# A forward and backward decode kernel: five wq chunks kept in SBUF, w1's place lent to other loads, w2's chunks released one step earlier

## The chip, the cores and the metric

The kernel runs on one core of one Trainium2 chip. The metric is the time of one execution on the device in microseconds (us); lower is better. A run's profile is one execution, taken by the hardware profiler.

## What is computed

Two attention layers A and two dense layers B alternate, for one token, and the gradient of all of it with respect to the input, both caches and all weights is computed as well. Both attention layers use the same wq, wo and caches, and both dense layers the same w1, b1 and w2, so every gradient of a weight is a sum over two layers.

```python
# D = 1024, Hq = 32, Hkv = 4, Dh = 128, Sk = 32768, F = 3584; all bfloat16
def A(x, k_cache, v_cache, wq, wo):
    W = 4096                                  # only the last 4096 positions are read
    q = x @ wq
    p = softmax(q . k[Sk-W:] * Dh ** -0.5)
    return (p @ v[Sk-W:]) @ wo                # wq: D x 4096, wo: 4096 x D
def B(x, w1, b1, w2):
    h = x @ w1 + b1
    return (h * tanh(softplus(h))) @ w2       # w1: D x F, w2: F x D
x = x + A(ln(x)); x = x + B(ln(x)); x = x + A(ln(x)); x = x + B(ln(x))
# outputs: x, then grad_out pulled back to x, k_cache, v_cache, wq, wo, w1, b1, w2
```

Of the gradients of the caches only the last 4096 of 32768 positions differ from zero. The rest, 56 pieces of 1 MiB, is written as zeros.

## The kernel before

**Stages.** The order is: transposes of K and attention forward 0 (`attn_fwd`), dense forward 0 (`mlp_fwd`, then a loop over the seven chunks of w2 with `mlp_out`), attention forward 1, dense forward 1, then backward: `dn_b1` (through w1 of layer B1), `attn_bwd(1)`, a loop over w2's seven chunks that does the forward product of layer B1 and the backward product of layer B0 together, `dn_b0`, `attn_bwd(0)`, and last the gradients of all weights and caches (`units_rows`, `units_cols`, `units_kv`), which are computed from short rows and written out. The program's order on each engine is written by hand.

**Chunks and the ring.** wq has 8 chunks, wo 8, w2 7, each 1 MiB; w1 has 8 tiles of 0.875 MiB. K's four groups and V's four are 1 MiB each. `Ring` (L38) holds 8 slots of 1 MiB. `want` puts a load at the end of one list; `pump` issues loads from the head of the list on SP's queue as long as there is a free slot, and stops at the first that finds none; `release` frees a slot and pumps. A load with a place of its own (`own`) takes no slot. A key such as ("2", 0, 3) names chunk 3 of w2 for use 0; the text writes it 2(0,3). wq is used four times (q(0,t) and q(1,t) forward, q(2,t) and q(3,t) backward), wo three times (o(0,c), o(1,c), o(3,c)), w2 twice. `keep` renames a slot's chunk to its next use, so that it isn't loaded again: KEEP_Q for q(1,t), KEEP_Q2 for q(3,t).

**Turning.** A backward product needs a weight's blocks transposed. `turned` (L426) does it in place: 8 PE transposes (L431) into PSUM, a copy back by ACT or DVE (`evac`, L284 and L287), and later the product itself (L443). `later` and `flush` delay the products: up to two (in attn_bwd up to six) stay open behind the newest transposes. A row may instead be multiplied on DVE (`rowdot`, L408). In `rows_chunk` two of the four rows of a w2 chunk go to DVE, two are turned. A chunk of q(2,t) that is kept for q(3,t) stays turned.

**Zeros.** `zeros(n, after)` issues n of the 56 zero writes on GpSimd's queue (POOL, L248). With `after` it first copies one element of that tile, so that POOL waits for it; what comes later on POOL waits too.

**Results.** In the last stage `stage_free` is a list of 1 MiB places in which results are put together before SP stores them (L967, L972). They are the third of w1's place that is left over (3 places), then V's and K's places and the ring's.

Of the kernel before, what the change touches and what calls it, by code (L numbers as in the profile page):

```python
# [15 lines left out]
P = 128  # L16
HQ = 32
DH = 128
D = 1024
J = 4096  # L20
F = 3584
G = 4
W = 4096
TD = D // P
TF = F // P
TS = W // P
SLOT = 4096
# [10 lines left out]
class Ring:  # L38
# [6 lines left out]
        self.pending = deque()  # L45
        self.where = {}

    def want(self, key, src, shape, own=None):
        self.pending.append((key, src, shape, own))

    def pump(self):
        while self.pending:
            key, src, shape, own = self.pending[0]
            if own is None:
                if not self.free:
                    return
                s = self.free.popleft()
                n = 1
                for k in shape[1:]:
                    n *= k  # L60
                dst = self.slots[s][:, 0:n]
                if len(shape) == 3:
                    dst = dst.rearrange("p (a b) -> p a b", a=shape[1])
                self.where[key] = (s, dst)
            else:
                dst = own
            self.pending.popleft()
            self.nc.sync.dma_start(dst, src)

# [6 lines left out]

    def release(self, key):
        s, _ = self.where.pop(key)
        self.free.append(s)
        self.pump()  # L80


# [1 line left out]
def kernel(  # L84
# [50 lines left out]
    W1 = sb([P, TD, F], BF16, "W1")  # L135
# [55 lines left out]
    DQC = sb([P, HQ, 2], BF16, "DQC")  # L191
# [14 lines left out]
    ring = Ring(nc, [ring_t[:, i, :] for i in range(8)])  # L206
    wq_v = A_wq.rearrange("(t p) j -> p t j", p=P)

    wo_v = A_wo.rearrange("(c p k) d -> p c k d", p=P, k=4)
# [3 lines left out]
    def kv_src(cache, g):  # L213
        return cache[0, g, ZR:, :].rearrange("(p t) d -> p t d", p=P)
# [2 lines left out]
        for t in ts:  # L217
            ring.want(("q", k, t), wq_v[:, t, :], [P, J])

    def want_o(k, cs=range(8)):  # L220
        for c in cs:
            ring.want(("o", k, c), wo_v[:, c], [P, 4, D])

    def want_2(k, cs=range(7)):
        for c in cs:
# [14 lines left out]
    def zeros(n, after=None):  # L240

        if after is not None and zjobs:
            nc.gpsimd.tensor_copy(pz[0:1, pz_n[0] % 16:pz_n[0] % 16 + 1], after[0:1, 0:1])
            pz_n[0] += 1
        for _ in range(n):
            if zjobs:
                dst = zjobs.pop()
                nc.gpsimd.dma_start(dst, zt[:])  # L248


    KEEP_Q = (6, 7)
    KEEP_Q2 = (5, 6, 7)
    EARLY_2 = (0, 1)
    for g in range(G):
        ring.want(("K", g), kv_src(A_k_cache, g), [P, TS, P])
    want_q(0)
    for g in range(G):
        ring.want(("V", g), kv_src(A_v_cache, g), None, own=VS[:, g])
    want_2(0, EARLY_2)
    want_o(0)  # L260
    for t in range(TD):
        ring.want(("1", t), w1_v[:, t, :], None, own=W1[:, t, :])
    want_2(0, [c for c in range(7) if c not in EARLY_2])
    want_q(1, [t for t in range(8) if t not in KEEP_Q])
    want_o(1)
# [157 lines left out]
    def flush():  # L423
        while lag:
            lag.popleft()[1]()
# [169 lines left out]
    def mlp_fwd(l, x, st):  # L595
        name = f"B{l}"
        n32, rstd = ln_fwd(x, st, NB[:, :, l], name)
        h_ps = MV[:, 192:192 + TF]
        for t in range(TD):
            for fb in range(TF):  # L600
                nc.tensor.matmul(h_ps[:, fb:fb + 1], lhsT=f_block(W1[:, t], fb), rhs=NB[:, t, l:l + 1],  # L601
                                 start=(t == 0 and fb == 0), stop=(t == TD - 1), skip_group_check=True)

        taken = []

        def col(n):
            if n == "mp":
                return sb([P, TF], FP32, f"{n}_{name}")
            taken.append(n)
            return mlp_t[:, (len(taken) - 1) * TF:len(taken) * TF]  # L610

        h, nh, z, w, m, om, A, B, num, den, t_, = (col(n) for n in "h nh z w m om A B num den t".split())
        V = nc.vector
        V.tensor_tensor(out=h[:], in0=h_ps, in1=b1c[:], op=ALU.add)

        V.scalar_tensor_tensor(out=nh[:], in0=h[:], scalar=-1.0, in1=h[:], op0=ALU.mult, op1=ALU.min)
        nc.scalar.activation(z[:], nh[:], ACT.Exp)
        nc.scalar.activation(w[:], nh[:], ACT.Exp, scale=2.0)
        V.tensor_scalar(out=m[:], in0=h[:], scalar1=0.0, scalar2=None, op0=ALU.is_ge)
        V.tensor_scalar(out=om[:], in0=h[:], scalar1=0.0, scalar2=None, op0=ALU.is_lt)  # L620
        V.tensor_tensor(out=A[:], in0=m[:], in1=w[:], op=ALU.max)
        V.tensor_tensor(out=B[:], in0=om[:], in1=w[:], op=ALU.max)
        V.scalar_tensor_tensor(out=num[:], in0=z[:], scalar=2.0, in1=A[:], op0=ALU.mult, op1=ALU.add)
        V.scalar_tensor_tensor(out=den[:], in0=B[:], scalar=2.0, in1=num[:], op0=ALU.mult, op1=ALU.add)
        V.reciprocal(den[:], den[:])
        V.tensor_tensor(out=t_[:], in0=num[:], in1=den[:], op=ALU.mult)
        if l == 0:
            V.tensor_tensor(out=AC[:, :, l], in0=h[:], in1=t_[:], op=ALU.mult)

        def deriv():  # L630

            mp, sg, s2 = col("mp"), col("sg"), col("s2")
            V.tensor_scalar(out=s2[:], in0=z[:], scalar1=1.0, scalar2=None, op0=ALU.add)
            V.reciprocal(s2[:], s2[:])
            V.tensor_tensor(out=sg[:], in0=m[:], in1=z[:], op=ALU.max)
            V.tensor_tensor(out=sg[:], in0=sg[:], in1=s2[:], op=ALU.mult)
            V.tensor_tensor(out=mp[:], in0=t_[:], in1=t_[:], op=ALU.mult)
            V.tensor_scalar(out=mp[:], in0=mp[:], scalar1=-1.0, scalar2=1.0, op0=ALU.mult, op1=ALU.add)
            V.tensor_tensor(out=mp[:], in0=mp[:], in1=h[:], op=ALU.mult)
            V.tensor_tensor(out=mp[:], in0=mp[:], in1=sg[:], op=ALU.mult)  # L640
            V.tensor_tensor(out=mp[:], in0=mp[:], in1=t_[:], op=ALU.add)
            return mp

        def act_late():
            V.tensor_tensor(out=AC[:, :, l], in0=h[:], in1=t_[:], op=ALU.mult)

        return dict(n32=n32, rstd=rstd, deriv=deriv, act_late=act_late)

    def mlp_out(l, ch, c, y_ps):
        for tt in range(4):  # L650
            fb = 4 * c + tt
            for dd in range(TD):
                nc.tensor.matmul(y_ps[:, dd:dd + 1], lhsT=ch[:, tt, dd * P:(dd + 1) * P], rhs=AC[:, fb, l:l + 1],
                                 start=(fb == 0 and dd == 0), stop=(fb == TF - 1), skip_group_check=True)
# [37 lines left out]
            early_da(2 * c + 1)  # L692

    x1, st1, sA0 = attn_fwd(0, x0, st0, True, wo_hook0)
    sB0 = mlp_fwd(0, x1, st1)
    mp0 = sB0["deriv"]()
    y_ps = MV[:, 256:256 + TD]
    mv_open()
    for c in range(7):
        ch = ring.get(("2", 0, c))  # L700
        mlp_out(0, ch, c, y_ps)
        if c in EARLY_2:
            ring.release(("2", 0, c))
        elif c < 6:
            rows_chunk(ch, c, GB, 1, gbc, da1, DA)
            later(lambda c=c: ring.release(("2", 0, c)))
# [32 lines left out]
    x3, st3, sA1 = attn_fwd(1, x2, st2, False, wo_hook1, last_da)  # L739
    put_by("OC", OC, HQ)  # L740
    put_by("NA", NA, TD)
    zeros(7, x3)
    sB1 = mlp_fwd(1, x3, st3)
    put_by("NB", NB, TD)
    conv(8, "A")
# [175 lines left out]

    def dq3():
        w1_rest(2)
        zeros(3, DQC[:, 0, 1:2])

    def dn3(t):
        if t % 2:
            w1_rest(1)
        if t == 5:
            zeros(1, dnp[:, t:t + 1])  # L930

    g2 = attn_bwd(1, sA1, g3, ("o", 1), ("q", 2), KEEP_Q2,
                  dict(do=lambda c: conv(2), dp=dp3, dq=dq3, dn=dn3))


    W1S = W1[:].rearrange("p t f -> p (t f)")
    ROWS = W1S[:, 0:5120]
    NOFF = 1024
    rf = W1S[0:7, 5120:6144]
# [3 lines left out]
    DOST = W1S[:, 11008:11264]  # L943

    TWIN = W1S[:, 11264:16384]
    stage_free = deque(W1S[:, 16384 + i * SLOT:16384 + (i + 1) * SLOT] for i in range(3))
    rt_n = [0]

    def rowize(cols, n, base, off):
# [118 lines left out]


    nc.vector.tensor_copy(GB[:, :, 0], g2[:])  # L1070
    zeros(3, g2)
    bcast(lambda c: GB[:, c, 0:1], TD)
    da0 = tmp([P, HQ], FP32, "da")
    y_ps = MV[:, 384:384 + TD]
# [2 lines left out]
    for c in range(7):  # L1077
        ch = ring.get(("2", 1, c))
        mlp_out(1, ch, c, y_ps)
        rows_chunk(ch, c, GB, 0, LB[0], da0, DA)  # L1080
        later(lambda c=c: ring.release(("2", 1, c)))
    flush()
# [3 lines left out]
    w1_rest(len(w1_units))  # L1086
    zeros(2, dh0)
    g1 = dn_b0(g2)
    nc.vector.tensor_copy(GA[:, :, 0], g1[:])
    zeros(2, g1)  # L1090

    x4 = sb([P, TD], BF16, "x4")
    nc.vector.tensor_tensor(out=x4[:], in0=y_ps, in1=x3[:], op=ALU.add)
# [8 lines left out]
    def do1(c):  # L1102
        if c == 0:
            rowize(GA, TD, 32, 0)
        if c == 3:
            todo[1].append(units_rows(32, HQ, out_5))
        if c == 5:
            store_rows(x4[:], TD, out_0[0, 0, :])
            store_f(db)
        if c == 5:  # L1110
            zeros(1, do1_acc[:, 4 * c:4 * c + 1])

    def dp1():
        zeros(4)
# [7 lines left out]

    def dn1(t):
        if t in (3, 6, 7):
            zeros(2 if t < 7 else 1, dnp[:, t:t + 1])
        if t == 4:
            twins()
        if t == 5:
            todo[0].append(units_cols(0, 8, out_4))
# [9 lines left out]
    nc.vector.tensor_copy(g0b[:], g0[:])  # L1139
    store_rows(g0b[:], TD, out_1[0, 0, :])  # L1140
    stage_free.extendleft(ring_t[:, i, :] for i in range(8))

    way.close()
    late = ctx.enter_context(tc.tile_pool(name="late", bufs=1, space=bass.MemoryType.PSUM))
# [42 lines left out]
```

## Time and profile before

| | before |
|---|---|
| time, median of 3 runs (lowest, highest) | 461.11 us (460.48, 461.47) |
| span of the profiled execution | 460.6 us |
| busy share: PE, PE weight load, DVE, ACT, POOL | 73%, 60%, 57%, 50%, 8% |
| moved by DMA | 183.59 MB, 399 GB/s on average |
| of it zero writes on POOL's queue | 58.72 MB |
| read from HBM, written to it | 83.94 MB, 98.62 MB |

The profiled execution's own time is not given apart from its span; the median of the three runs is 0.5 us above that span. "PE" is the matrix engine, "DVE" the vector engine, "ACT" the scalar engine, "SP" the queue that issues most DMAs. In a timeline a row is: start, duration, engine, line, operation, output and input, count, and in brackets the idle time before it and what ended it. In a row of a window follow its length, the busy time (and count) of PE, PE's weight loads, DVE, ACT and POOL, then the granted clock of PE, the share of DMA time and GB/s.

### The profile page before, as it was taken

The page shows a single profiled execution, that of the slowest core. Times are in us where ns is not written, and L with a number is a line of the kernel's source. Part 1 is how long each engine was busy: PE and PEld are TensorE (multiplying, and loading weights), DVE is VectorE, ACT ScalarE, POOL GpSimd, SP SyncE. Part 2 cuts the span into 40 slices and gives each one's busy share as a digit, 9 for nine tenths or more (in the row PEclk, how much of TensorE's full clock was granted, in tenths as well). Part 3 has the DMA queues.
Part 4 walks back from the last instruction along what each step waited for, and adds up shares of the span by engine and source line. Part 5 has one row for each costly group of instructions (what it writes and reads, how often), then busy time and mean ns, then how long its engine had stood idle before and what let it go on. Part 6 is the DMA issues. An engine that isn't in the chain of part 4 may idle for free. (4 is left out here: it accounts for less than half of the span.)

```text
span 460.6 us, 14273 instructions
## 1 busy us (share of the span) xinstructions
PE 337.2 (73%) x6385; PEld 275.3 (60%) x6385; DVE 261.3 (57%) x517; ACT 228.2 (50%) x263; POOL 38.6 (8%) x85
## 2 busy tenths in 40 slices
PE   4836435597678788599879898897896876677950
PEld 3736435497668787599779898787791121112530
DVE  6505731383150149678428786475485987878860
ACT  2502001064035369378128573283267988778850
POOL 4000000000111320100210101102111000000000
PEclk9955555555555569799559855597595555555555
DMA  8999999999999999999999999979999999999995
GB/s 340 420 419 419 419 420 416 422 388 392 393 422 424 418 414 414 406 384 386 376 424 334 407 387 371 414 264 408 424 420 421 419 425 421 427 424 419 408 407 227
DMA packets 28379, 183.59 MB, mean 399 GB/s; under 512 B 3706, under 2 KB 3734, under 8 KB 9494
## 3 DMA queue, kind: packets, MB, share of 16 engines
q1 hardware_dynamic: 20162, 123.94, 67.0%
q0 software_dynamic: 8064, 58.72, 30.7%
q8 instruction: 50, 0.82, 0.7%
q14 instruction: 11, 0.09, 0.0%
q10 hardware_dynamic: 92, 0.02, 0.0%
HBM read 83.94 MB, written 98.62 MB: 396 GB/s over the span
## 5 line engine op out<-in xcount | busy, mean ns | idle before, releaser
L287 ACT COPY ring<-BIG 128x1024 bf16<-128x1024 bf16 x73 | 72.2, 1013 | 40.4 <-PE BIG L431 37.7
L431 PE MATMUL BIG<-ident_bf,ring 128*128 128x128 bf16 x872 | 80.0, 252 | 3.8 <-DMA ring<-in_A_wo_dram 2.0
L431 PEld LDWEIGHTS <-ring 128*128 128x128 bf16 x952 | 69.8, 114 | 5.2 <-DMA ring<-in_A_wo_dram 2.3
L995 PE MATMUL wide<-W 2*128 2x512 bf16 x228 | 48.5, 601 | 19.0 <-DVE ring L284 3.6
L408 DVE CUSTOM_DVE_ANT_0 junk<-ring,SC 128x1024 bf16<-128x1024 bf16 x38 | 46.2, 1216 | 4.5 <-DMA ring<-in_A_wo_dram 1.7
L995 PEld LDWEIGHTS <-W 2*128 2x128 bf16 x240 | 10.9, 103 | 54.5 <-issue 53.8
L443 PEld LDWEIGHTS <-ring 128*128 128x128 bf16 x1024 | 38.2, 100 | 4.6 <-ACT ring L287 4.4
L287 ACT COPY KT<-BIG 128x1024 bf16<-128x1024 bf16 x22 | 21.8, 1015 | 32.3 <-PE BIG L582 30.9
L287 ACT CAST ring<-wide 128x1024 bf16<-128x1024 f32 (+1 forms) x38 | 35.2, 998 | 4.9 <-PE wide L995 4.0
L284 DVE COPY ring<-BIG 128x1024 bf16<-128x1024 bf16 x36 | 24.8, 691 | 20.3 <-PE BIG L431 13.1
L284 DVE CAST ring<-wide 128x1024 bf16<-128x1024 f32 (+1 forms) x26 | 30.2, 1200 | 5.7 <-PE wide L995 5.2
L248 POOL DMA_DIRECT2D out_dram<-zt x56 | 29.6, 534 | 6.3 <-DMA out_dram<-zt 5.6
L553 PE MATMUL MV<-OC,ring 128*128 128x1 bf16 x512 | 16.6, 166 | 15.2 <-DMA ring<-in_A_wo_dram 12.6
L287 ACT COPY W<-BIG 128x1024 bf16<-128x1024 bf16 x20 | 18.9, 1151 | 15.7 <-PE BIG L766 15.7
L553 PEld LDWEIGHTS <-ring 128*128 128x128 bf16 x512 | 16.0, 106 | 16.0 <-DMA ring<-in_A_wo_dram 13.2
L284 DVE CAST VS<-wide 128x1024 bf16<-128x1024 f32 (+1 forms) x18 | 21.0, 1190 | 4.1 <-PE wide L995 3.1
L473 PE MATMUL MV<-NA,ring 128*128 128x1 bf16 x512 | 15.0, 165 | 10.9 <-DMA ring<-in_A_wq_dram 10.0
L601 PE MATMUL MV<-NB,W 128*128 128x1 bf16 x448 | 16.2, 172 | 9.2 <-DMA W<-in_B_w_dram 6.5
L408 DVE CUSTOM_DVE_ANT_0 junk<-ring,DSX 128x1024 bf16<-128x1024 bf16 x18 | 22.0, 1224 | 0.6
L601 PEld LDWEIGHTS <-W 128*128 128x128 bf16 x448 | 15.9, 118 | 9.8 <-DMA W<-in_B_w_dram 7.2
L1046 PE MATMUL wide<-W 32*128 32x256 bf16 x128 | 20.4, 403 | 1.4 <-ACT W L287 0.8
L473 PEld LDWEIGHTS <-ring 128*128 128x128 bf16 x512 | 14.3, 103 | 11.6 <-DMA ring<-in_A_wq_dram 10.6
(256 smaller groups left out, 539.1 us busy)
## 6 DMA issues: line engine op xcount, KB each, us to landing
out_dram<-zt POOLq DMA_DIRECT2D x56, 1024.0 KB, 12.7
ring<-in_A_wq_dram SPq DMA_DIRECT2D x27, 1024.0 KB
ring<-in_A_wo_dram SPq DMA_DIRECT2D x24, 1024.0 KB
ring<-in_B_w_dram SPq DMA_DIRECT2D x14, 1024.0 KB
out_dram<-ring SPq DMA_DIRECT2D x9, 1024.0 KB
W<-in_B_w_dram SPq DMA_DIRECT2D x8, 896.0 KB
ring<-in_A_k_cache_dram SPq DMA_DIRECT2D x4, 1024.0 KB
VS<-in_A_v_cache_dram SPq DMA_DIRECT2D x4, 1024.0 KB
```

Of the source, the lines that this page charges most:

```text
L248: nc.gpsimd.dma_start(dst, zt[:])
L284: nc.vector.tensor_copy(dst, src)
L287: nc.scalar.copy(dst, src)
L408: nc.vector.tensor_tensor_reduce(out=out, in0=a, in1=vec, scale=1.0, scalar=acc if i else 0.0, op0=ALU.mult, op1=ALU.add, accum_out=acc)
L431: nc.tensor.transpose(b[:, i * P:(i + 1) * P], block(w, i) if block else w[:, i * P:(i + 1) * P], ident_bf[:])
L443: nc.tensor.matmul(out, lhsT=w[:, i * P:(i + 1) * P], rhs=rhs_of(i), start=fresh[0], stop=last and i == n - 1, skip_group_check=True)
L473: nc.tensor.matmul(q_ps[:, h:h + 1], lhsT=ch[:, h * P:(h + 1) * P], rhs=NA[:, t, l:l + 1], start=(t == 0 and h == 0), stop=(t == TD - 1), ...
L553: nc.tensor.matmul(y_ps[:, dd:dd + 1], lhsT=ch[:, tt, dd * P:(dd + 1) * P], rhs=OC[:, h, l:l + 1], start=(h == 0 and dd == 0), stop=(h == ...
L601: nc.tensor.matmul(h_ps[:, fb:fb + 1], lhsT=f_block(W1[:, t], fb), rhs=NB[:, t, l:l + 1], start=(t == 0 and fb == 0), stop=(t == TD - 1), ...
L995: nc.tensor.matmul(b[:, 512 * i:512 * i + 512], lhsT=R[at:at + 2, lo:lo + P], rhs=R[at:at + 2, ro + 512 * i:ro + 512 * i + 512], start=Tru ...
L1046: nc.tensor.matmul(b[:, k * 256:(k + 1) * 256], lhsT=RT[32 * g:32 * g + 32, a, tp, :], rhs=YS[32 * g:32 * g + 32, :], start=True, stop=Tru ...
```

## The change

It has four parts.

1. Five chunks of wq (3 to 7) are kept between q(0) and q(1), and between q(2) and q(3); before it was two (6, 7) and three (5, 6, 7).
2. w1's place (7 MiB, as much as seven slots) takes K's four groups and then o(0,0) to o(0,6) at the start. A tile of w1 is loaded when the chunks of wo that lie under it are released (`over`). After `dn_b0` w1 is not needed any more, and three slots' worth of its place are added to the ring (`lend`); the results get them back at the end.
3. In both loops over w2's chunks a `flush()` follows the forward product of each chunk. So the open products of the chunk before are done, and that chunk is released, before the new chunk's transposes begin.
4. Zero writes are placed otherwise: one behind the arrival of w1's last tile, one more after attention forward 1, one more in each of two places of attn_bwd(1), two less ahead of the backward w2 loop, none after g1 (two before), and within attn_bwd(0) one more at c == 5 and one less at t == 6. Their number stays 56.

```diff
-    def want(self, key, src, shape, own=None):
-        self.pending.append((key, src, shape, own))
+    def want(self, key, src, shape, own=None, over=()):
+        self.pending.append((key, src, shape, own, over))
 
     def pump(self):
         while self.pending:
-            key, src, shape, own = self.pending[0]
-            if own is None:
+            key, src, shape, own, over = self.pending[0]
+            if any(k in self.where for k in over):
+                return
+            if own is not None:
+                self.where[key] = (None, own)
+                dst = own
+            else:
                 if not self.free:
                     return
...
     def release(self, key):
         s, _ = self.where.pop(key)
-        self.free.append(s)
+        if s is not None:
+            self.free.append(s)
+        self.pump()
+
+    def lend(self, slots):
+
+        self.free.extend(range(len(self.slots), len(self.slots) + len(slots)))
+        self.slots.extend(slots)
         self.pump()
...
-    def want_o(k, cs=range(8)):
+    def want_o(k, cs=range(8), homes=()):
         for c in cs:
-            ring.want(("o", k, c), wo_v[:, c], [P, 4, D])
+            own = homes[c].rearrange("p (k d) -> p k d", k=4) if c < len(homes) else None
+            ring.want(("o", k, c), wo_v[:, c], [P, 4, D], own, [("K", c)] if own is not None else [])
...
-    KEEP_Q = (6, 7)
-    KEEP_Q2 = (5, 6, 7)
+    KEEP_Q = (3, 4, 5, 6, 7)
+    KEEP_Q2 = (3, 4, 5, 6, 7)
     EARLY_2 = (0, 1)
+    W1S = W1[:].rearrange("p t f -> p (t f)")
+    homes = [W1S[:, i * SLOT:(i + 1) * SLOT] for i in range(7)]
     for g in range(G):
-        ring.want(("K", g), kv_src(A_k_cache, g), [P, TS, P])
+        ring.want(("K", g), kv_src(A_k_cache, g), None, own=homes[g].rearrange("p (t d) -> p t d", t=TS))
...
-    want_o(0)
+    want_o(0, homes=homes)
     for t in range(TD):
-        ring.want(("1", t), w1_v[:, t, :], None, own=W1[:, t, :])
+        under = [("o", 0, i) for i in range(7) if i * SLOT < (t + 1) * F and (i + 1) * SLOT > t * F]
+        ring.want(("1", t), w1_v[:, t, :], None, own=W1[:, t, :], over=under)
...
     x1, st1, sA0 = attn_fwd(0, x0, st0, True, wo_hook0)
+    zeros(1, W1[:, TD - 1, 0:1])
     sB0 = mlp_fwd(0, x1, st1)
...
         ch = ring.get(("2", 0, c))
         mlp_out(0, ch, c, y_ps)
+        flush()
         if c in EARLY_2:
             ring.release(("2", 0, c))
...
-    zeros(7, x3)
+    zeros(8, x3)
...
-        zeros(3, DQC[:, 0, 1:2])
+        zeros(4, DQC[:, 0, 1:2])
...
-        if t == 5:
+        if t in (3, 5):
             zeros(1, dnp[:, t:t + 1])
...
-    stage_free = deque(W1S[:, 16384 + i * SLOT:16384 + (i + 1) * SLOT] for i in range(3))
+    lent = [W1S[:, 16384 + i * SLOT:16384 + (i + 1) * SLOT] for i in range(3)]
+    stage_free = deque()
...
-    zeros(3, g2)
+    zeros(1, g2)
...
         ch = ring.get(("2", 1, c))
         mlp_out(1, ch, c, y_ps)
+        flush()
         rows_chunk(ch, c, GB, 0, LB[0], da0, DA)
         later(lambda c=c: ring.release(("2", 1, c)))
...
     g1 = dn_b0(g2)
+    ring.lend(lent)
     nc.vector.tensor_copy(GA[:, :, 0], g1[:])
-    zeros(2, g1)
...
-            zeros(1, do1_acc[:, 4 * c:4 * c + 1])
+            zeros(2, do1_acc[:, 4 * c:4 * c + 1])
...
-            zeros(2 if t < 7 else 1, dnp[:, t:t + 1])
+            zeros(2 if t == 3 else 1, dnp[:, t:t + 1])
...
     stage_free.extendleft(ring_t[:, i, :] for i in range(8))
+    stage_free.extendleft(lent)
```

More of the change, by code (lines that the diff above doesn't have):

```diff
@@ L64, in pump @@
                 self.where[key] = (s, dst)
-            else:
-                dst = own
             self.pending.popleft()
@@ L933 @@
                   dict(do=lambda c: conv(2), dp=dp3, dq=dq3, dn=dn3))
-    W1S = W1[:].rearrange("p t f -> p (t f)")
     ROWS = W1S[:, 0:5120]
```

## The prediction

> **What bounds the kernel now.** I read the page's DMA rows first, then SP's timeline (which load is issued when), then PE's timeline (who waits for a load), then the windows of five microseconds.
>
> The page, rows 2, 3 and 6:
> ```profile
> DMA  8999999999999999999999999979999999999995
> GB/s 340 420 419 419 419 420 416 422 388 392 393 422 424 418 414 414 406 384 386 376 424 334 407 387 371 414 264 408 424 420 421 419 425 421 427 424 419 408 407 227
> DMA packets 28379, 183.59 MB, mean 399 GB/s; under 512 B 3706, under 2 KB 3734, under 8 KB 9494
> ...
> out_dram<-zt POOLq DMA_DIRECT2D x56, 1024.0 KB, 12.7
> ring<-in_A_wq_dram SPq DMA_DIRECT2D x27, 1024.0 KB
> ```
> The DMA engines look full from end to end. But 56 of the 175 MiB are zero writes that nothing waits for: they are issued where the program has put them, and fill whatever the loads leave. So a full DMA row does not say that the loads set the pace.
>
> SP's timeline, the stretches that the change touches:
> ```profile
> 71.48 20.08 SPq L68 DMA_DIRECT2D ring<-in_B_w_dram  x5
> 92.08 18.34 SPq L68 DMA_DIRECT2D ring<-in_A_wq_dram  x6
> ...
> 244.28 25.42 SPq L68 DMA_DIRECT2D ring<-in_B_w_dram  x7
> 272.36 10.63 SPq L68 DMA_DIRECT2D ring<-in_A_wo_dram  x5
> ...
> 301.38 4.45 SPq L68 DMA_DIRECT2D ring<-in_A_wo_dram  x3
> ```
> PE's timeline in the same stretches (products of w2 are L653, of wq L473, transposes L431):
> ```profile
> 90.21 2.70 PE L653 MATMUL MV<-AC,ring 128*128 128x1 bf16 x96 [2.41 <-DVE AC L628]
> ...
> 103.43 0.99 PE L653 MATMUL MV<-AC,ring 128*128 128x1 bf16 x32
> ...
> 109.87 4.41 PE L473 MATMUL MV<-NA,ring 128*128 128x1 bf16 x160
> 115.62 1.55 PE L473 MATMUL MV<-NA,ring 128*128 128x1 bf16 x52 [1.34 <-DMA ring<-in_A_wq_dram]
> ...
> 260.67 0.95 PE L653 MATMUL MV<-AC,ring 128*128 128x1 bf16 x32
> ...
> 310.91 0.62 PE L431 MATMUL BIG<-ident_bf,ring 128*128 128x128 bf16 x8 [0.62 <-DMA ring<-in_A_wo_dram]
> ...
> 314.40 0.62 PE L431 MATMUL BIG<-ident_bf,ring 128*128 128x128 bf16 x8 [1.40 <-DMA ring<-in_A_wo_dram]
> ```
> Up to 86.7 us PE follows the loads. From 90 to 345 it waits for a load only in the three rows marked here, 3.4 us together: that whole stretch is a chain of computation. The last part is bound by DMA again, as the windows show: a dip at 300, full from there to 455, while the last evacuation (chain of waits: DVE VS L284, 444.05 and 1.22 long) ends at 445.3.
> ```profile
> 300.00:305.00 5.00, 5.00 (x133) 5.00 (x131) 4.04 (x8) 4.55 (x5) 0.00 (x0) 1.00 0.56 186
> 305.00:310.00 5.00, 4.48 (x112) 4.21 (x110) 3.81 (x7) 4.18 (x6) 0.70 (x2) 1.00 0.96 329
> ...
> 450.00:455.00 5.00, 0.00 (x0) 0.00 (x0) 0.00 (x0) 0.00 (x0) 0.00 (x0) 0.50 0.94 379
> ```
>
> **What goes.** wq is loaded 8+3+8+3 = 22 times instead of 27: 5 MiB, 5.24 MB, 12.5 us at 420 GB/s. None of it is waited for directly except q(1,5) at 115.62. The zero writes stay 56. Until w1 has landed (85.4 us) the same 33 MiB of loads are ahead of PE, so the first 90 us stay; w1's wait for o(0,c) costs nothing, since PE reads o(0,c) at 52 to 70 us and w1's turn in the DMA queue comes from 68 on.
>
> **What comes: three free slots in the forward w2 stage.** Five of eight slots hold wq, two hold 2(0,0) and 2(0,1), one holds o(0,7) and then 2(0,2). So 2(0,3) is issued only when 2(0,0) is released, 91.23 (today's issue of 2(0,6)), and each later load waits for a release. The price of a load from issue to use: 5.5 us, from q(1,5), issued at 110.09 and used at 115.62. Today fwd3 (the product of chunk 3) starts at 94.43, fwd6 at 103.43, 3.0 per chunk. Rows used: a product 0.9, a row's transposes 0.83 (two rows 1.65), a product of a turned row 0.27, ACT's copy of one 1.01.
> - fwd3 waits for 91.2+5.5 = 96.7; its flush ends at 98.2 and releases 2(0,2), so 2(0,5) is usable at 103.7.
> - Turning chunk 3 ends at 99.9, fwd4 at 100.8. The flush then waits for ACT's second copy (101.2): 101.6. 2(0,6) is usable at 107.2.
> - fwd5 waits until 103.7, flush to 105.1, q(1,0) usable at 110.7. fwd6 waits until 107.2: 3.8 later than today.
> - q(1,2) gets the slot of 2(0,6): 110.09+3.8 = 113.9, usable at 119.4. PE takes q0 and q1 before, then six products of 0.88: 124.7 against 119.4 today. **+5.3 us.**
> Even with loads that are never waited for, the flush costs 0.4 per chunk, because PE waits for ACT's second copy before it goes on: about +2.4 at fwd6. POOL's new wait on W1's last tile holds up nothing: its next instruction is the copy of QC at 119.66, 33 us later, and the one zero write it releases is over by about 92.5.
>
> **The same in the backward w2 stage.** Today fwd0 is at 260.67 and the last product ends at 282.6. 2(1,0..2) come with the releases of q(2,0..2), in time. With the flush, 2(1,3) is issued at 265.0 and usable at 270.5, where turning chunk 2 ends at 269.7: fwd3 waits 0.8. The flush costs 0.4 on each of six chunks, 2.4, and the waits that are not inside it add 0.6: **+3.0 us.** g1 (292.4) comes 8.3 us later, with 5.3 and 3.0.
>
> **What comes back.** After g1, w1's three slots take o(3,3..5) at once, so the waits at 310.91 and 314.40 go: **-2.0.** Chunks 3 and 4 of wq are already turned in the last dn loop: 6 times 0.45 us of PE transposes, and as many evacuations; DVE, which ends that loop (dnp at 346.6), has some 3 of them less, 0.69 each: **-2.3.** So g0 comes 8.3-4.3 = 4.0 us later. SP's new loads stand behind the rf copies (293.82, end 294.5) and ahead of rowize's two copies; nobody waits for those before 330.
>
> **The end.** From g1 on both kernels have the same bytes to move: 8 loads, 14 zeros, 38 MiB of results (o(3,3..7) and q(3,0..2) now, o(3,5..7) and q(3,0..4) before). They begin at 302.4 today (SP's 301.38 and 1.0), at 294.5+8.3+1.0 = 303.8 after: +1.4. From 302 to 315 today's loads come one by one and lose some 1.2 us in the two rows above; three at once should not: -1.2. So DMA by itself ends 0.2 later. But the results are computed 4.0 later, 3.8 behind DMA's own shift. How much of that the queue covers is not shown directly. The thinnest place I find is SP's pause from 429.5 (row at 425.60) to 431.74, 2.2 us, which DMA outlasts at a share of 1.02. Ends: all covered, +0.2; nothing covered, +4.0. I take 2.1 covered, plus 0.5 to restart: +0.2+1.7+0.5 = **+2.4.** Span 460.6+2.4 = 463.0. The timed median is 461.11, 0.5 above the span: **463.5 us.**
>
> The Trainium skill ("DMA: Bandwidth & Descriptors", Anatomy of one DMA) gives a lone transfer a fixed 2.0 us plus its bytes over 436 GB/s: 4.4 us for 1 MiB, an estimate from that page, against the 5.5 of the row. With 4.4 the two stages would cost about 2.7 each instead of 5.3 and 3.0, and the same sum would come to 460.6. The row had another load just ahead of it, so both are possible; it says either way that loads issued one by one do not run at 420 GB/s.
>
> **Rivals.**
> 1. *Bytes decide*, faster. If DMA is what every stage waits for, 5.24 MB at 420 GB/s go: 461.1-12.5 = 448.6. For it: the DMA row. Against: PE's three waits of 3.4 us in all from 90 to 345. Chance 0.05. The Trainium skill ("Perfetto Trace Analysis", Identifying the Most-Contended Engine) says to improve the engine with the highest occupancy first, which here would be DMA; PE's 3.4 us of waits do not bear that out so far.
> 2. *The starved stages cost half*, faster. Without waits for single loads only the flushes cost: +2.4 less the 1.3 that PE waits at 115.62 today, and +2.4: g1 +3.5, g0 -0.8. DMA's last stretch starts at 299.0, 3.4 earlier, 4.6 with the loss made good; the slip against it is 3.8 as before, 2.2 uncovered: -2.4, 458.7; 456.5 if the queue covers all of it. It decides from a shift of g1 under about 6 us. For it: the issue-to-use price comes from one row. Chance 0.28.
> 3. *A zero write gets in front of a starved load*, slower by more. Today 2(1,5), issued at 266.39, is used only at 275.06 (DVE waits 1.58 for it), 8.7 us, with three zero writes of 260.24 in the queue. With three slots each such meeting is paid in full: 3.2 us more than 5.5, once in each w2 stage, adds 6.4 to 463.5, less what the queue covers: 467 to 470. Against: only one zero write is left at each place. Chance 0.17.
> The forecast keeps 0.50, with 461.0 to 466.0 for itself. A measurement here can tell about 0.2%, 0.9 us. Under 460.2 lie rival 1, 0.24 of rival 2 and 0.05 of the forecast: 0.34. Within 0.2%: 0.04 and 0.10, 0.14. Over 462.0: 0.35 and rival 3, 0.52. Leaving out rival 1, a little of rival 2 below and the end of rival 3 gives 456.5 to 469.0.
>
> **What would show it.** Right: 22 wq loads; w2's loads in SP's timeline one by one 3 to 4 us apart; L653 rows from 94 on with waits for ring<-in_B_w of 1 to 2.5 us; L490 at 125 instead of 119.65; DMA windows clearly under 420 GB/s in 92 to 120 and 270 to 300; no wait for wo around 310 to 320; dnp's last rowdot 2 us closer to its start. Wrong: L490 under 122 and g1 under 298 (rival 2), or DMA idle in the last 100 us for more than 5 us, which would mean that computation sets the end alone.

## The result, and the profile after

The changed kernel takes 467.57 us (median of four runs, 466.22 to 469.03) against 461.29 us: 1.0141 times as long, 95% interval 1.0110 to 1.0172. The forecast was slower, 463.5 us in a range of 456.5 to 469.0; the time lies in that range, but above the 461.0 to 466.0 that the forecast kept for itself. The profiled execution's span is 466.5 us, 5.9 more than the 460.6 of before; it moved 5.26 MB less.

The page of the changed kernel, the same rows as before:

```profile
DMA  8999999886999999999999968999999999899997
GB/s 337 424 418 419 422 416 420 324 314 222 398 393 367 405 405 407 417 411 384 405 413 420 400 225 321 320 343 360 422 422 419 413 398 404 341 415 417 408 405 316
DMA packets 27658, 178.33 MB, mean 382 GB/s; under 512 B 3626, under 2 KB 3654, under 8 KB 9414
...
ring<-in_A_wq_dram SPq DMA_DIRECT2D x20, 1024.0 KB
```

The bytes went as planned: 20 loads of wq into the ring and two into w1's place are the 22 of the change. But the DMA row is no longer full. It has two holes, in slices 8 to 10 (82 to 117 us: 324, 314, 222 GB/s) and in slices 24 to 28 (268 to 327 us). In the first, w2's chunks and then wq's come through three slots. The second begins in the backward w2 stage, which ends at 295, and goes on behind it.

SP's timeline of the changed kernel (start, duration of the merged row, load, count):

```profile
71.51 30.48 SPq L71 DMA_DIRECT2D ring<-in_B_w_dram  x5
104.93 10.86 SPq L71 DMA_DIRECT2D ring<-in_A_wq_dram  x3
...
252.42 32.42 SPq L71 DMA_DIRECT2D ring<-in_B_w_dram  x7
287.83 7.24 SPq L71 DMA_DIRECT2D ring<-in_A_wo_dram  x3
...
304.82 1.52 SPq L71 DMA_DIRECT2D W<-in_A_wo_dram  x3
```

Five loads of w2 now take 30.5 us to be issued instead of 20.1, and wq's first for layer 1 goes out at 104.9 instead of 92.1. The last row is the lending: three chunks of wo into w1's place, issued together right after `dn_b0`.

PE's timeline (the products of w2 are now L667, of wq L487):

```profile
96.66 1.01 PE L667 MATMUL MV<-AC,ring 128*128 128x1 bf16 x32 [1.95 <-DMA ring<-in_B_w_dram]
...
100.15 1.01 PE L667 MATMUL MV<-AC,ring 128*128 128x1 bf16 x32 [0.32 <-DMA ring<-in_B_w_dram]
...
108.80 1.01 PE L667 MATMUL MV<-AC,ring 128*128 128x1 bf16 x32 [2.21 <-DMA ring<-in_B_w_dram]
...
120.30 4.11 PE L487 MATMUL MV<-NA,ring 128*128 128x1 bf16 x148 [3.21 <-DMA ring<-in_A_wq_dram]
126.57 1.31 PE L487 MATMUL MV<-NA,ring 128*128 128x1 bf16 x44 [2.16 <-issue]
128.16 1.98 PE L504 MATMUL SC<-QC,KT 128*128 128x8 bf16 x69 [0.28 <-DVE QC L494]
```

A chain that waited for one load of wq now waits for three of w2 and for one of wq. The first score product of layer 1 starts at 128.16 instead of 119.65, 8.5 us later. In the kernel before, the end of the same chain was:

```profile
118.06 1.31 PE L473 MATMUL MV<-NA,ring 128*128 128x1 bf16 x44 [0.89 <-issue]
119.65 2.38 PE L490 MATMUL SC<-QC,KT 128*128 128x8 bf16 x84 [0.28 <-DVE QC L480]
```

"issue" marks a stop of PE for which the trace shows nothing that PE waits for. It grew from 0.89 to 2.16 us.

The windows show the idle DMA beside it, and what is left of the last stretch:

```profile
95.00:100.00 5.00, 3.17 (x64) 2.90 (x64) 2.47 (x4) 1.81 (x3) 0.00 (x0) 0.50 0.78 272
110.00:115.00 5.00, 2.92 (x35) 2.48 (x32) 3.59 (x13) 3.58 (x5) 0.00 (x0) 0.50 0.67 218
...
305.00:310.00 5.00, 5.00 (x46) 4.68 (x47) 1.38 (x2) 1.55 (x2) 0.00 (x0) 0.51 0.83 276
...
405.00:410.00 5.00, 4.16 (x19) 0.82 (x16) 5.00 (x5) 4.51 (x5) 0.00 (x0) 0.50 0.77 310
```

The row at 405 is new in kind: before, no window between 315 and 450 fell under a share of 1.00. Now DMA runs dry while results are still being computed, since those come later.

The same points of the program in all profiled executions (us; one execution each, while the times are medians). "QC" is POOL's copy of QC, right behind the wq products of layer 1. "w2 back" is the time from g_A to dh on POOL's timeline, the backward w2 stage. "g1" is the second of the two copies of g1 into GA on DVE (the first is 0.25 earlier). "last" is the end of the last evacuation.

| kernel | KEEP_Q, KEEP_Q2 (chunks) | flush | QC | w2 back | g1 | last | span | time |
|---|---|---|---|---|---|---|---|---|
| before | 2, 3 | no | 119.7 | 23.1 | 292.7 | 445.3 | 460.6 | 461.3 |
| changed | 5, 5 | yes | 128.2 | 26.4 | 304.8 | 457.3 | 466.5 | 467.6 |
| e1 | 2, 5 | yes | 121.1 | 26.0 | 296.7 | 448.6 | 457.6 | 460.4 |
| e2 | 5, 3 | yes | 128.2 | 25.3 | 306.0 | 459.4 | 469.3 | 470.7 |
| e3 | 2, 3 | yes | 120.6 | 25.4 | 296.0 | 447.4 | 457.4 | 461.1 |
| e4 | 2, 3 | no | 120.7 | 23.3 | 295.0 | 447.3 | 457.5 | 459.5 |
| e5 | 5, 5 | no | 128.4 | 28.4 | 309.1 | 463.3 | 472.5 | 473.7 |
| e6 (no lending) | 2, 3 | yes | 120.8 | 25.0 | 296.7 | 448.5 | 464.2 | 465.1 |
| e7 | 2, 4 | no | 121.5 | 23.3 | 296.1 | 448.1 | 457.3 | 457.7 |
| e9 | 4, 5 | yes | 120.9 | 26.0 | 298.2 | 453.1 | 462.3 | 461.6 |
| e10 (kept chunks first) | 5, 5 | yes | 122.6 | 28.4 | 299.6 | 451.9 | 461.1 | 463.3 |
| e11 (kept chunks first) | 2, 4 | no | 119.5 | 23.6 | 294.2 | 445.1 | 455.0 | 457.8 |

### The profile page after: what moved, and what is told of

The parts are those of the page before. It is cut to its first block, busy times and chain, and to the rows that moved or that the text cites. A ratio compares the mean times of both kernels' runs of the same rounds, so it can differ in the third digit from the quotient of the medians.

```text
span 466.5 us, 14146 instructions
## 1 busy us (share of the span) xinstructions
PE 337.0 (72%) x6337; PEld 271.6 (58%) x6337; DVE 260.1 (56%) x515; ACT 224.0 (48%) x259; POOL 38.7 (8%) x86
## 5 line engine op out<-in xcount | busy, mean ns | idle before, releaser
L301 ACT COPY ring<-BIG 128x1024 bf16<-128x1024 bf16 x62 | 60.6, 1014 | 44.0 <-PE BIG L445 35.3
L445 PE MATMUL BIG<-ident_bf,ring 128*128 128x128 bf16 x720 | 65.8, 257 | 1.5 <-ACT W L301 1.1
L445 PEld LDWEIGHTS <-ring 128*128 128x128 bf16 x776 | 59.5, 117 | 2.5 <-issue 1.9
L422 DVE CUSTOM_DVE_ANT_0 junk<-ring,SC 128x1024 bf16<-128x1024 bf16 x34 | 41.3, 1216 | 6.2 <-DMA ring<-in_B_w_dram 4.6
L298 DVE CAST ring<-wide 128x1024 bf16<-128x1024 f32 (+1 forms) x29 | 33.8, 1201 | 9.0 <-PE wide L1011 5.5
L457 PEld LDWEIGHTS <-ring 128*128 128x128 bf16 x896 | 30.7, 99 | 11.5 <-ACT ring L301 7.0
L301 ACT CAST ring<-wide 128x1024 bf16<-128x1024 f32 (+1 forms) x35 | 33.1, 1000 | 4.3 <-PE wide L1011 2.7
L301 ACT COPY W<-BIG 128x1024 bf16<-128x1024 bf16 x28 | 26.7, 1112 | 16.2 <-PE BIG L782 15.3
L298 DVE COPY ring<-BIG 128x1024 bf16<-128x1024 bf16 x28 | 19.3, 691 | 17.7 <-PE BIG L445 10.7
L487 PE MATMUL MV<-NA,ring 128*128 128x1 bf16 x512 | 15.0, 165 | 13.8 <-DMA ring<-in_A_wq_dram 11.7
L487 PEld LDWEIGHTS <-ring 128*128 128x128 bf16 x512 | 14.3, 103 | 14.5 <-DMA ring<-in_A_wq_dram 12.3
L301 ACT CAST KT<-wide 128x1024 bf16<-128x1024 f32 x20 | 20.2, 1022 | 4.2 <-PE wide L1011 3.1
L422 DVE CUSTOM_DVE_ANT_0 junk<-W,SC 128x512 bf16<-128x512 bf16 (+1 forms) x20 | 15.8, 792 | 6.8 <-PE SC L325 6.1
```

The lines of the kernel that those rows point to most:

```text
L298: nc.vector.tensor_copy(dst, src)
L301: nc.scalar.copy(dst, src)
L422: nc.vector.tensor_tensor_reduce(out=out, in0=a, in1=vec, scale=1.0, scalar=acc if i else 0.0, op0=ALU.mult, op1=ALU.add, accum_out=acc)
L445: nc.tensor.transpose(b[:, i * P:(i + 1) * P], block(w, i) if block else w[:, i * P:(i + 1) * P], ident_bf[:])
L457: nc.tensor.matmul(out, lhsT=w[:, i * P:(i + 1) * P], rhs=rhs_of(i), start=fresh[0], stop=last and i == n - 1, skip_group_check=True)
L487: nc.tensor.matmul(q_ps[:, h:h + 1], lhsT=ch[:, h * P:(h + 1) * P], rhs=NA[:, t, l:l + 1], start=(t == 0 and h == 0), stop=(t == TD - 1), ...
```

## The experiments

Three theories were set against each other: A, three slots are too few for the time from a load's issue to its use; B, the new places of the zero writes and of the loads in w1's place; C, the flush itself. All edits are to the changed kernel unless said otherwise.

**Which kept set costs (e1, e2, e3).**

```diff
# e1
-    KEEP_Q = (3, 4, 5, 6, 7)
+    KEEP_Q = (6, 7)
# e2
-    KEEP_Q2 = (3, 4, 5, 6, 7)
+    KEEP_Q2 = (5, 6, 7)
# e3: both
```

> KEEP_Q is (6, 7) again, all else as in the changed kernel: six slots serve the forward w2 stage instead of three, and 3 MiB more are loaded. Theory A (the starved slots make the slip): the first score product of layer 1, 128.2 in the changed kernel and 119.7 before, comes back to about 121 (the flush keeps some 1 to 2 us), g1 about 6 us earlier than in the changed kernel, time 461 to 463. Theory B (the new places of zero writes, and w1's place for other loads, make it): no change, 467 plus the added loads. Theory C (the flush makes it, PE waiting for ACT's copies): score product stays near 127, time 466 to 468.

> KEEP_Q2 is (5, 6, 7) again, all else as in the changed kernel: five slots for the backward w2 stage, 2 MiB more loaded, two chunks of wq turned again in the last dn loop. Theory A: the backward stage (first w2 product to the last product of the stage) takes about 24 us instead of the changed kernel's 24.9 and the 21.9 of before, because most of its loss was the flush; the last dn loop is about 2 us longer again; together 466 to 468. Theory B: 467. Theory C: stage stays at 24 to 25, time 468 to 469.

> Both sets of kept chunks as before; lending, flushes and zero places as in the changed kernel. Theory A: forward slip gone but for 1 to 2 us, backward stage 24: g1 about 4 us after that of before instead of 12, time 460 to 462. Theory B: 466 to 468. Theory C: 466 to 468.

e1 took 460.40 us, 0.9972 of the kernel before (0.9940 to 1.0003): with 3 MiB more to load it is 7 us faster than the changed kernel, and the copy of QC is back from 128.2 to 121.1. It lies 0.6 below A's range. The loss is made by the chunks kept through the forward w2 stage. e2 took 470.70 us (1.0184, 1.0138 to 1.0229), more than any theory said; its QC stays at 128.2. Its backward stage is 1.1 shorter than the changed kernel's, but its last dn loop takes 18.7 us instead of 15.6. So keeping five chunks in the backward half does not hurt, and undoing it saves nothing. e3 took 461.08 us (0.9985, 0.9959 to 1.0012), at the middle of what A expected. B falls: all that it blames is in e1 and e3 as well. C falls as the whole cause: e1 and e3 have the flushes.

**Without kept chunks and flushes (e4).**

```diff
# e3, and in both loops over w2's chunks
         mlp_out(0, ch, c, y_ps)
-        flush()
```

> As the one before, and both flushes taken out: what is left of the change is w1's place for other loads and the new places of the zero writes. Theory A: g1 where it was before, within 1 us; the two waits for wo after g1 (2.0 us) gone; DMA starts its last stretch 6 us earlier than before: 456 to 459, faster than the kernel before. Theory B: 466 to 468, since all that it blames is still there. Theory C: also 456 to 459; A and C are told apart by the runs above.

459.47 us, 0.9952 (0.9923 to 0.9982): lending and the new zero places alone are faster than the kernel before, by less than the 2 to 5 us of A's range. The backward stage is 23.3 us, 2.1 less than with the flush (e3). g1 came 2.3 later than before, where I expected 1 at most; that slip lies in the dn loop of attn_bwd(1) (from the copy of DQC's element to that of g_A 30.9 us instead of 28.4), in which the change places two more zero writes (part 4). PE's stops for "issue" ahead of the products there (L457) are 1.6 us in e4, and none is listed before. The changed kernel, with the same zero writes, takes 28.2 there, and no run takes them back alone; what makes the slip stays open.

**Without the flushes, with five kept chunks (e5).**

```diff
         mlp_out(0, ch, c, y_ps)
-        flush()
...
         mlp_out(1, ch, c, y_ps)
-        flush()
```

> The changed kernel with both flushes taken out; five chunks stay kept in both places. Theory A (three slots are too few for the time from a load's issue to its use): a slot is now released one pair of turns (1.65 us) later, so each load comes later and both w2 stages get longer: the copy of QC, 128.2 in the changed kernel, at 130 to 131; the backward stage (26.4 from g_A to dh on POOL's timeline) at 26 to 28; time 469 to 472. Theory C (the flush itself is the cost): both stages shorter, time 463 to 465.

473.68 us (1.0257, 1.0200 to 1.0315), 6 us slower than with them, so C's rule, shorter without the flush, does not hold with three slots. In the profiled execution the last evacuation comes 6.0 later; the backward stage, 28.4 us, makes 2.0 of it, and the dn loop of attn_bwd(1) and the stretch after g1, which the edit does not touch, make 1.8 and 1.5. The same backward code as in the changed kernel also took 28.4 once (e10), so that these 2.0 come from the flush is not shown. My number for the forward stage was wrong: QC stays at 128.4. PE's timeline of e5, and SP's below it, show why:

```profile
108.22 1.01 PE L667 MATMUL MV<-AC,ring 128*128 128x1 bf16 x32 [0.67 <-DMA ring<-in_B_w_dram]
...
117.68 1.01 PE L487 MATMUL MV<-NA,ring 128*128 128x1 bf16 x32 [2.02 <-DMA ring<-in_A_wq_dram]
120.61 4.11 PE L487 MATMUL MV<-NA,ring 128*128 128x1 bf16 x148 [1.91 <-DMA ring<-in_A_wq_dram]
...
91.33 12.20 SPq L71 DMA_DIRECT2D ring<-in_B_w_dram  x4
107.63 7.59 SPq L71 DMA_DIRECT2D ring<-in_A_wq_dram  x3
```

The last product of w2 is at 108.22 (108.80 with the flushes), and the products of wq behind it go on after 120.61 (120.30). The last load of w2 is issued 1.5 earlier with the flushes (101.66 against 103.20), but takes 7.1 us to its use instead of 5.0. What the flush gained in lead went into a longer load, so the forward stage comes out even.

**A threshold or a proportion (e9).**

```diff
-    KEEP_Q = (3, 4, 5, 6, 7)
+    KEEP_Q = (4, 5, 6, 7)
```

> The changed kernel with KEEP_Q (4, 5, 6, 7): four slots in the forward w2 stage, one more MiB loaded. Theory A, with a threshold at the time from issue to use: one slot more gives each load 3.4 us more lead, so nearly all waits go, the copy of QC at 122 to 123 instead of 128.2, time 461 to 463. Rival D, loss in proportion to the chunks kept (2 kept: 121.1, 5 kept: 128.2): 125 to 126, 464 to 466.

461.56 us (1.0005, 0.9977 to 1.0033). QC is at 120.9, as good as with two kept chunks: one slot more takes back all that the three further kept chunks cost, not a third of it. PE's timeline of e9:

```profile
104.35 1.04 PE L667 MATMUL MV<-AC,ring 128*128 128x1 bf16 x32
...
116.10 4.52 PE L487 MATMUL MV<-NA,ring 128*128 128x1 bf16 x160 [2.50 <-DMA ring<-in_A_wq_dram]
```

The last product of w2 is at 104.35, and PE waits for no load in the whole stage; before it was at 103.43. A wait for wq of 2.50 stays, and the stop for "issue" does not appear. So of the 7.3 us that QC gains, 4.4 are the loads of w2, 0.7 those of wq and 2.2 that stop. Rival D, the proportion, is out.

**The wait for q(1,2) (e10).**

```diff
-        for t in range(TD):
+        order = list(range(TD)) if l == 0 else list(KEEP_Q) + [t for t in range(TD) if t not in KEEP_Q]
+        for t in order:
...
-                                 start=(t == 0 and h == 0), stop=(t == TD - 1), skip_group_check=True)
+                                 start=(t == order[0] and h == 0), stop=(t == order[-1]), skip_group_check=True)
```

> The changed kernel, but the wq products of layer 1 begin with the five kept chunks and take q(1,0) to q(1,2) last. Nothing else changes. Theory A: the wait of 3.2 us for q(1,2) at 120.3 is covered by five products of 0.88, and the kept chunks' slots come free earlier: the copy of QC at 124 to 125, time 463 to 465. Theory C and B see no reason for a change: 467.

463.27 us (1.0039, 1.0005 to 1.0073), 4.3 less than the changed kernel; QC at 122.6, better than the 124 to 125 expected:

```profile
113.07 5.79 PE L488 MATMUL MV<-NA,ring 128*128 128x1 bf16 x212
120.98 1.31 PE L488 MATMUL MV<-NA,ring 128*128 128x1 bf16 x44 [2.12 <-issue]
```

The wait for wq is gone from PE. That the products also began 2.2 earlier (113.07, not 115.25) is w2's last load being used after 1.8 us less wait, which this edit does not explain. Its backward stage was 28.4 us, longer than the 26.4 of the same code in the changed kernel and the 26.0 of e1 and e9; PE's waits for w2 in it are 3.1 us. Loads one by one are not steady.

**The flush by itself (e6): the kernel before with the two lines added.**

```diff
         mlp_out(0, ch, c, y_ps)
+        flush()
...
         mlp_out(1, ch, c, y_ps)
+        flush()
```

> The kernel before, with the two flushes added and nothing else. Theory A with the prediction's price of a flush (0.4 us a chunk, PE waiting for ACT's second copy): the backward w2 stage, 23.1 from g_A to dh on POOL's timeline, at 25.2 to 25.7; the forward one 1 us longer at most, since PE waits for q(1,5) behind it anyway; g1 2 to 3 us later, and time 461.5 to 464, the DMA queue covering a part. If the flush cost nothing on its own and only helped, the stage would stay at 23.1 and the time at 461.

465.05 us (1.0069, 1.0040 to 1.0098), 1 us above the range. The backward stage takes 25.0 instead of 23.1, a little under the range; POOL's timeline of e6:

```profile
262.11 0.18 POOL L243 COPY pz<-g_A 1x1 f32<-1x1 f32 x1 [7.83 <-DVE g_A L397]
287.07 0.19 POOL L243 COPY pz<-dh 1x1 f32<-1x1 f32 x1 [23.16 <-DVE dh L1086]
```

QC is 1.1 later and g1 4.0, where 2 to 3 was expected. Here, without lending, the end moves by 3.6: DMA's last stretch begins with SP's issue at 305.2 instead of 301.4, and the end follows it.

**A version that beats both (e7, e11).**

```diff
-    KEEP_Q = (3, 4, 5, 6, 7)
-    KEEP_Q2 = (3, 4, 5, 6, 7)
+    KEEP_Q = (6, 7)
+    KEEP_Q2 = (4, 5, 6, 7)
...
-        flush()        # in both loops
# e11: and the kept chunks first, as in e10
```

> KEEP_Q (6, 7), KEEP_Q2 (4, 5, 6, 7), no flushes: four slots for the backward w2 stage. Theory A: with four slots a load is issued 6 us ahead of its product even without the flush, more than the 5.5 that it takes; the backward stage stays at 23 to 24 (23.3 in the run with the keeps and flushes undone), one chunk less is turned in the last dn loop (about 1 us) and 1 MiB less is loaded than there: 456.5 to 459. If a stage with fewer slots is starved whatever the lead, the stage goes to 25 or more and the time to 460 to 462.

> The fastest version so far (KEEP_Q (6, 7), KEEP_Q2 (4, 5, 6, 7), no flushes) with the wq products of layer 1 beginning with the two kept chunks. Theory A: the wait for the last loaded chunk (2.5 us at most there) is partly covered by two products of 0.88: the copy of QC about 1 us earlier than its 121.5, time 456 to 458; no change if that wait moves to the last chunk whole.

e7 took 457.67 us, 0.9929 of the kernel before (0.9909 to 0.9950), and 10 us less than the changed kernel. With four slots and no flush the backward stage is 23.3 us, as with five. e11 brought QC to 119.5, 2.0 earlier than e7, and 457.77 us (0.9923, 0.9897 to 0.9948): no difference to e7 in the time, though its profiled span, 455.0, is the shortest of all; that execution was the fastest of its six.

## Why the prediction was right, and where its terms were off

**Direction and mechanism: shown.** The forecast said that the bytes do not set the pace of the middle, that three slots starve both w2 stages, and that this costs more than it brings back. e1 loads 3 MiB more and is faster; e9 removes PE's waits for w2 with one slot. That is the forward half. In the backward half three slots cost the stage about 1 us (26.4 against 25.3 in e2) and the kept chunks bring back more than that. Rival 1 is out by the sign. (The section of the Trainium skill that the prediction names there, "Perfetto Trace Analysis", Identifying the Most-Contended Engine, has DMA judged by its use of HBM bandwidth and not by occupancy; with 5.26 MB less to move the kernel got slower either way.) Rival 2 is out by QC at 128.2 and g1 at 304.8 (it needed under 122 and 298). Rival 3 is not what happened in the forward stage: POOL issued its one zero write at 87.4 and the next at 128.3, and the first starved load took 5.4 us, inside the price. The backward stage rose by 3.3 us, which leaves no room for its further 3.2.

**The size: partly luck.** The forecast is +2.4 and the measured change +6.3 (+5.9 in the span). The time lies in rival 3's 467 to 470, and inside the stated range only because the range was widened for that rival. Two errors also work against each other: the last evacuation came 12.0 later where 4.0 was forecast, but the queue covered 6.1 of it where 2.1 was taken. From stretch to stage the 12.0 are 8.5 (forward), 0.3, 3.3 (backward), -2.3 (after g1), 1.1 (DOC to DQC), -1.8 (last dn loop) and 2.9 (last stage).

**Forward stage: +5.3 forecast, +8.5 measured.** The steps held up to fwd5: fwd3 forecast 96.7, measured 96.66; fwd4 99.9 and 100.15; fwd5 103.7 and 103.11. Then fwd6, forecast 107.2, came at 108.80: the load issued at 101.66 took 7.1 us to its use, not 5.5. The next one that PE waits for, q(1,2), took 4.8 (115.46 to 120.30), so only 0.9 of that slip was left at 120.30, where 119.4 was forecast. The larger part of the 3.2 missing us is the stop for "issue": 2.16 us, 44 matmuls before the end of the wq products. The forecast's six products of 0.88 have no such stop, although the trace of before shows one of 0.89 there. So two terms were mis-sized: the stop, put at nothing, and the price of one load, taken from one row and used as a constant, where this trace has 5.4 (91.30 to 96.66), 7.1 and 4.8. The Trainium skill ("DMA: Bandwidth & Descriptors", Anatomy of one DMA) gives a transfer issued by GpSimd a time from which 4.4 us for 1 MiB is an estimate; the three measured here, issued by SP, lie 0.4 to 2.7 above that, so with 4.4 the forecast loss would have been further off.

**Backward stage: +3.0 forecast, +3.3 measured** (26.4 against 23.1). Of it the flush is 2.1 (e3 against e4) or 1.9 (e6 against before), where 2.4 was forecast; the rest is the short waits. The same backward code took 26.0 in e1 and e9 and 28.4 in e10, so agreement to 0.3 is more than one execution can show. g1 came 12.1 later instead of 8.3: 3.2 of the difference from the forward stage, 0.3 from this one, 0.3 from what lies between.

**What comes back.** Forecast -2.0 in the stretch after g1, measured -2.3 (g1 12.1 later, the copy of DOC 9.8 later), and no product waits for wo there. The last dn loop, from the copy of DQC's element to the last of dnp, took 15.6 instead of 17.4: -1.8 for -2.3. Between the two, from DOC to DQC, 1.1 was lost, 1.0 of it a stop of PE for "issue" (L873) that is not there before. And a step was missing behind them. From the last dnp to the last evacuation the changed kernel takes 101.6 us, the kernel before 98.7; the five kernels with KEEP_Q2 of five chunks take 100.9 to 101.7, the two with four 99.6, those with three 98.7 to 99.5. So the dn loop's gain is given back in the last stage. A part of it shows on ACT: it copies the first result behind that loop 1.2 us before the last dnp in the kernel before (345.42), and 0.3 after it in the changed kernel (355.99), after 6.84 us idle. Counted from the copy of DQC's element that is 0.4 sooner, while the last dnp is 1.8 sooner; so 1.4 of the 2.9 is DVE's gain that did not reach ACT's results. What makes the rest was not tried and stays open.

**The end: +2.4 forecast, +5.9 measured.** The rule, that DMA's queue covers a part of the slip, held; its inputs were too small. The last evacuation came 12.0 later, the end 5.9, so 6.1 were covered. From the last evacuation to the end of the span it is 15.3 us before and 15.7 in e6, the two kernels without lending and without the new zero places, and 9.0 to 10.2 in all the others. So before, the queue was behind by some 6 us when computing ended, and in the others the end follows the last evacuation. Lending and the new zero places were not tried one without the other, so which of them does it is open. The forecast named DMA idle for more than 5 us in the last 100 as a sign that computation sets the end alone; in the changed kernel the windows from 370 to 460 add up to some 2.6 us idle, so the sign as it was worded did not clearly come. The term "-1.2", three loads at once running faster, did not come either: in the 20 us from the first of these loads DMA moved 353 GB/s before (from 301.4) and 344 in the changed kernel (from 304.8).

## What to carry to other kernels

A kept chunk costs a slot in every stage that it lives through, so the price of keeping is read there and not from the bytes: compare the lead (from the release that issues a load to the product that needs it) with the time from issue to use. In the forward stage here one slot decided over some 7 us: PE waited for three loads of w2 with three slots and for none with four. The same three slots cost the backward stage about 1 us, so the comparison has to be made stage by stage. A DMA row that is full does not say that fewer bytes help, if much of it is filler that could go elsewhere: ask which waits of the engines end with a load.

## What the runs showed that I had not expected

The time from a load's issue to its use is not a constant: 4.8, 5.4 and 7.1 us in one execution for the same 1 MiB. The load of 7.1 was not alone: q(1,0) was issued 3.3 us behind it, and from 103 to 110 DMA moved 1.96 MB, nearly two chunks. That alone does not settle it, for in e10 the same load, with the next as close behind it, took 5.3 (101.32 to 106.61) and in e2 6.9 (101.59 to 108.48). What sets it stays open. Plan with the longest, not with one row.

An earlier release did not bring the forward stage forward: without the flush the last load of w2 is issued 1.5 us later, and the stage still ended where it did (QC 128.4 and 128.2).

PE's stop for "issue", 44 matmuls before the end of layer 1's wq products, was 2.16 us in the changed kernel, 2.10 in e5, 2.12 in e10, 1.95 in e2, 1.61 in e11, 0.89 before and 0.67 in e6; e1, e3, e4, e7 and e9 have none. In those five PE waits for loads for 2.0 to 3.7 us in the 116 matmuls ahead of that place; before and in e6 it waits there for 1.34 and 1.85; in the others it does not wait there at all. So the stop and the waits look as if they ran side by side, and a load wait of up to some 2 us just ahead of such a stop costs little. That is a pattern in twelve executions; what the stop is, these runs don't show.
